# Three chains of A's second output moved between the merges of B's weights

## The chip, the cores and the metric

The kernel runs on one core of one Trainium2 chip. The metric is the device time of one execution in microseconds (us), the median of three runs. Matrix work runs on TensorE (PE in the profile), which writes PSUM banks; ScalarE (ACT) and VectorE (DVE) read these banks and write SBUF; GpSimd (POOL) masks the attention weights in SBUF; SyncE (SP) issues the DMAs.

## The reference

Two independent attention blocks over 2048 tokens of width 640, with 32 heads of width 20; their outputs stand side by side.

```python
def _A_ref(x, wqkv, wo):           # sliding window, W = 256
    q, k, v = split(x @ wqkv)      # (head, token, 20) each
    scores = q @ k.T * 20 ** -0.5
    mask = (i - j >= 0) & (i - j < 256)
    p = softmax(where(mask, scores, -1e9))
    return heads_joined(p @ v) @ wo

def _B_ref(x, wqkv, wo):           # linear attention
    phi = lambda t: where(t > 0, t + 1, exp(t)) + 1e-6
    pq, pk = phi(q), phi(k)
    kv = sum_s(pk[s] outer v[s]);  z = sum_s(pk[s])
    o = (pq @ kv) / (pq @ z + 1e-6)
    return heads_joined(o) @ wo

return concatenate([a, b], axis=-1)
```

## The kernel before, in words

The tokens are cut into four superblocks of 512. Block A's attention is cut into 76 units, numbered 0 to 75 here (units 56 to 75 belong to the last superblock, number 3). A unit is one pass of this loop (L1121): `scores` (L773) multiplies q by k into the four PSUM banks of `S_ps`, ScalarE takes the exponential of all of it into `p`, and GpSimd masks `p`. There is one `S_ps`, so the next unit's scores begin when the exponential has read it. About two units later, for each group of four heads that is complete, `values` (L821) multiplies `p` by v into a bank; VectorE turns that bank (`T`, L847), and a deferred function (`rest`, L856) takes a reciprocal and writes the normalised rows `N` and `Nr`; for the last group of a superblock VectorE turns `Nr` too (L886).

The other matrix work, called the fill, is cut into chains: a chain is the group of matmuls that fills one bank, five for a 512-wide chain (`chain`, L268). Each chain has a due time in `plan`, in units; `fill_of` (L1095) sorts the list by due time and hands the matmuls out in that order. A unit is credited with a fixed number of columns, `rate` (L1119), which is (386520 - 13000 + 32 * 2200) / 76 = 5841; a unit that also does `values` is charged 2200 of them; `take` (L1106) stops at the first matmul at which the credit is used up, and the overdraft goes to the next unit. A chain can so be split by a unit's scores.

All chains, the merges, the denominators and the `values` products use one pool of four banks, named `dense`, taken in rotation: a chain gets the bank that the fourth product before it used, and its first matmul waits until that bank has been read. Who reads it:

- `evac` (L250) copies a bank to SBUF on ScalarE or VectorE. It keeps an account of work for each, `load["A"]` and `load["D"]`, in nominal columns: a copy of n columns adds n + 160, a unit's exponential 1900 to A, a `values` product 1500 to D, a quotient 1400 to D, a denominator 1200 to D, a phi 672 to A and 1700 to D; each unit takes 3000 off both (`pass_tile`, L246). A copy goes to ScalarE if A is less than D + 600, else to VectorE:

```python
to = "A" if load["A"] < load["D"] + AHEAD else "D"
```

- `phi` (L277) takes an exponential on ScalarE at once (L281), and later, when two more banks have begun, two VectorE operations (L285, L288) of which the second reads the bank.
- `b_den` (L709) adds its small constant on VectorE (L727) and then takes a reciprocal.

Each engine works its instructions in the order in which the program gives them out. The pieces that the change touches:

- `b_merge` (L664) multiplies B's summed key-value matrices by B's output weights: ten merges of two matmuls of 320 columns (L673), called merge 0 to merge 9 here, each counted as 640 columns. `b_out` needs them all.
- `a_out(s)` and `b_out(s)` (L892, L760) are the output projections of a superblock: four 512-wide chains, called aout s.0 to s.3 here, and a fifth, s.4, of twenty 128-wide matmuls (`tok_rows`, L472).
- `b_q(s)` (L687) gives five chains of phi(q), here bq s.0 to s.4. Its first call does what is left of the quotients of superblock s - 2 (`quotient(s - 2)`).
- `quotients(s)` (L742) lists four divisions on VectorE (L752), here quot s.0 to s.3. The unit loop takes one from the list in a unit without `values` (L1141), ahead of that unit's fill, and in the others only when the list is long or after unit 68 (L1138). Each is followed by a transposing DMA on SP into `oT_B`.
- `again_x(s)` reloads a superblock of B's x by DMA.

In the last unit, 75, the loop takes 2000 columns of fill, does `values` of group 6, gives out that group's `rest` at once, and then goes on with the fill (L1129 to L1142). After the loop come 5500 columns of fill, `values` of group 7, the PE transposes of `turn_last` (L896), what is left of the fill, and `a_out_last` (L911), the output of A's last superblock.

The due times, sorted, with the times in unit 56 and around it before the change: merges 0 to 9 at 46.34, 47.02 and so on in steps of 0.68 to 52.46; aout 1.0 to 1.4 at 50.66, 51.58, 52.5, 53.42, 54.34; bq 2.0 at 52.5; the denominator of superblock 1 at 53.05; bq 2.1 at 53.5. The work runs behind these due times: merge 5 comes in unit 56.

Of the kernel before, what the change touches and what calls it, by code (L numbers as in the profile page):

```python
# [92 lines left out]
def kernel(  # L93
# [12 lines left out]
    KT = D // P  # L106
# [128 lines left out]
    def settle(all=True):  # L235
        while posts and (all or posts[0][0] <= begun[0]):
            posts.pop(0)[1]()
# [78 lines left out]
    for c in range(KT):  # L316
        m = EXTRA * c
        while m < EXTRA * (c + 1):
            n = min(EXTRA * (c + 1) - m, DH - m % DH)
# [178 lines left out]
    def wo_proj(wt, base, oT, s, col0):  # L498
        osb = op.tile([P, TPS, D], BF16, name="osb")

        def done(tb, ps):
            if tb is None:
                evac(osb[:, :, SB:D], ps)
            else:
                evac(osb[:, tb, 0:SB], ps[:])

        yield from tok_rows(oT, wt, base, done)
        dst = out2[s * SB : (s + 1) * SB, col0 : col0 + D]
        soon(
            lambda: nc.sync.dma_start(out=dst.rearrange("(t p) n -> p t n", p=P), in_=osb[:]), 2  # L510
        )
# [152 lines left out]
    def b_merge():  # L664

        for c in range(KT):
            for lo in (0, D // 2):
                cols = slice(lo, lo + D // 2)
                ps = bank()
                for i in range(2):  # L670

                    at = PAD + (P - GD) * c - i * GD
                    nc.tensor.matmul(  # L673
                        ps[:, 0 : D // 2],
                        lhsT=kv_T[0:GD, c + i, at : at + P],
                        rhs=wo_sb["B"][0 : GH * DH, c + i, cols],
                        start=(i == 0),
                        stop=(i == 1),
                    )
                evac(w_sb["B"][:, c, D + lo : D + lo + D // 2], ps[:, 0 : D // 2], D // 2)  # L680
                yield End(D)
# [210 lines left out]
    def a_out(s):  # L892
        settle()
        yield from wo_proj(wo_sb["A"], 0, oT_A[s], s, 0)
# [137 lines left out]
    plan = []  # L1032

    def at(t0, t1, gen, n):
        for i in range(n):
            plan.append((t0 + (i + 0.5) / n * (t1 - t0), gen, i == n - 1))
# [6 lines left out]
    def parts(t0, t1, n, s):  # L1043
        do(t0, t1, [lambda tb=tb: load_part(n, s, tb) for tb in range(TPS)])
# [30 lines left out]
        at(td, td + 0.1, b_den(s), 1)  # L1075
        do(tx, tx, [lambda s=s: quotients(s)])
    at(46.0, 52.8, b_merge(), 2 * KT)
    for n, s, t0, t1 in (("A", 0, 44.5, 48.5), ("A", 1, 50.2, 54.8), ("B", 0, 54.8, 59.2),
                         ("B", 1, 60.2, 64), ("A", 2, 64.4, 68.2), ("B", 2, 69, 73),
                         ("B", 3, 73, 76)):  # L1080
        at(t0, t1, (a_out if n == "A" else b_out)(s), KT)
    for n, s, t0, t1 in (("B", 1, 5, 9), ("A", 2, 6, 12), ("B", 2, 14, 18), ("B", 3, 19, 25),
                         ("A", 3, 25.5, 33.5)):
        parts(t0, t1, n, s)
# [98 lines left out]
```

## Time and profile before

| | |
|---|---|
| median of three runs | 253.49 us (253.42 to 253.66) |
| profiled execution | 253.07 us |
| its span, first to last instruction | 251.3 us |
| PE busy | 246.6 us, 98% of the span |
| ACT busy | 197.2 us, 78% |
| POOL busy | 186.7 us, 74% |
| DVE busy | 166.9 us, 66% |
| granted TensorE clock | 1.000 |

The span is the time that the timeline's stamps cover; what lies around it in the execution's own time is 1.8 us. A row of a timeline gives the start, the time from the first start to the last end of the merged instructions, the engine, the source line, the operation, output and input, and the count; a number in brackets behind it is the idle time just ahead, with what ended it. A modelled matmul overlaps the next, so the pace of matmuls is read from starts, not from the lengths. Scores stand in the PE timeline under L787, `values` under L834, chains under L271, merges under L673, denominators under L716.

### The profile page before, as it was taken

The numbers are of one execution on the slowest core, as the hardware profiler recorded it, in microseconds if no ns is written. First come the engines' busy times: TensorE is split into PE (matmuls) and PEld (weight loads), VectorE is DVE, ScalarE is ACT, GpSimd is POOL, SyncE is SP. The second block draws the span as 40 slices with busy tenths as digits, with TensorE's granted clock in tenths as the row PEclk, the third lists the DMA queues.
The fourth block names the chain that finished last, engine by engine and source line by source line (L and its number), as shares of the span: only waits on it lengthen the run. The fifth ranks groups of instructions, "written<-read, shape, count | busy, mean of one in ns | idle before, by whom it ended". The sixth has DMA issues, their size and how long they took to land.

```text
span 251.3 us, 8779 instructions
## 1 busy us (share of the span) xinstructions
PE 246.6 (98%) x3730; PEld 141.6 (56%) x3730; DVE 166.9 (66%) x310; ACT 197.2 (78%) x194; POOL 186.7 (74%) x310
## 2 busy tenths in 40 slices
PE   8999999999999999999999999999999999999994
PEld 6644456467755455466545555556555565655573
DVE  1345678767654565686665766666888798859662
ACT  4486789889867788996568877889998998999542
POOL 1227897879877898686878979888887978999800
PEclk9999999999999999999999999999999999999999
DMA  7995597799640342996569394742967398779614
GB/s 219 332 251 156 117 202 135 181 268 140 97 97 3 96 142 37 244 268 163 69 146 154 90 192 78 181 56 46 188 112 159 89 185 173 114 166 143 195 57 154
DMA packets 68412, 37.04 MB, mean 147 GB/s; under 512 B 51605, under 2 KB 67349, under 8 KB 68373
## 3 DMA queue, kind: packets, MB, share of 16 engines
q1 hardware_dynamic: 67685, 35.67, 68.1%
q10 hardware_dynamic: 688, 0.82, 1.0%
q8 instruction: 29, 0.48, 0.8%
q14 instruction: 10, 0.08, 0.1%
HBM read 14.42 MB, written 9.83 MB: 96 GB/s over the span
## 4 chain that ended last, share of the span: by engine, by line
PE 92%; DVE 2%; DMA 2%; ACT 1%; issue 1%; SPq 0%; ACTq 0%
PE dense L271 52%; PE S_ps L787 11%; PE dense L834 9%; PE dense L562 9%; PE dense L406 7%; DMA wA<-in_A_wqkv_dram 2%; PE first L406 1%; PE dense L716 1%; PE dense L673 1%; PE dense L645 1%; DVE phi L288 1%; DVE e L285 0%; ACT e L281 0%; PE dense L901 0%; ACT osb L256 0%
## 5 line engine op out<-in xcount | busy, mean ns | idle before, releaser
L810 POOL TENSOR_SCALAR_AFFINE_SELECT p<-p 128x256 bf16<-128x256 bf16 (+2 forms) x280 | 176.9, 662 | 41.5 <-ACT p L795 40.0
L795 ACT ACTIVATE p<-S_ps 128x2048 bf16<-128x2048 f32 x76 | 142.8, 1879 | 33.8 <-PE S_ps L787 32.0
L271 PE MATMUL dense<-xA,wqk 128*128 128x512 bf16 x200 | 50.9, 380 | 0.0
L787 PEld LDWEIGHTS <-kpad 20*128 20x128 bf16 (+1 forms) x1216 | 21.7, 98 | 29.6 <-issue 26.0
L787 PE MATMUL S_ps<-qpad,kpad 20*65 20x64 bf16 (+3 forms) x1216 | 33.7, 228 | 0.0
L847 DVE STREAM_TRANSPOSE T<-dense 128x512 f32<-128x512 f32 x32 | 22.8, 712 | 15.6 <-PE dense L834 15.4
L285 DVE TENSOR_SCALAR e<-e 128x512 bf16<-128x512 bf16 x40 | 18.6, 465 | 21.4 <-ACT e L281 21.3
L271 PEld LDWEIGHTS <-wqk 128*128 128x128 bf16 x200 | 17.9, 98 | 19.2
L288 DVE SCALAR_TENSOR_TENSOR phi<-dense,e 128x512 bf16<-128x512 f32 x40 | 27.7, 692 | 1.6
L271 PE MATMUL dense<-xB,wB 128*128 128x512 bf16 x100 | 26.3, 380 | 0.0
L834 PE MATMUL dense<-p,vA 128*32 128x64 bf16 (+2 forms) x1216 | 25.9, 231 | 0.0
L271 PE MATMUL dense<-wB,xB 128*128 128x512 bf16 (+1 forms) x160 | 25.9, 300 | 0.0
L562 PE MATMUL dense<-tok,phi 128*128 128x129 bf16 (+1 forms) x160 | 25.5, 300 | 0.0
L271 PE MATMUL dense<-wo,oT 128*128 128x512 bf16 (+4 forms) x165 | 25.1, 296 | 0.0
L281 ACT ACTIVATE e<-dense 128x512 bf16<-128x512 f32 x40 | 23.6, 597 | 1.2 <-PE dense L271 1.0
L271 PE MATMUL dense<-wB,xA 128*128 128x512 bf16 (+1 forms) x160 | 24.3, 299 | 0.0
L406 PE MATMUL dense<-wA,xA 128*128 128x320 bf16 x140 | 23.7, 299 | 0.2 <-DMA wA<-in_A_wqkv_dram 0.2
L834 PEld LDWEIGHTS <-vA 128*32 128x32 bf16 x1216 | 19.4, 97 | 3.8 <-issue 0.8
L256 ACT ACTIVATE osb<-dense 128x512 bf16<-128x512 f32 (+2 forms) x28 | 15.8, 580 | 5.3 <-PE dense L271 5.2
L406 PEld LDWEIGHTS <-xA 128*128 128x128 bf16 x160 | 14.9, 98 | 8.0 <-DVE xA L347 0.4
L864 DVE TENSOR_TENSOR N<-T,recA 128x320 bf16<-128x320 f32 (+1 forms) x28 | 15.5, 553 | 3.3 <-DMA oT<-N 2.3
L752 DVE TENSOR_TENSOR tok<-tok,rden 128x640 bf16<-128x640 bf16 x16 | 17.5, 1093 | 0.2 <-DMA tok<-phi 0.2
(65 smaller groups left out, 195.8 us busy)
## 6 DMA issues: line engine op xcount, KB each, us to landing
out_dram<-osb SPq DMA_DIRECT2D x7, 640.0 KB
x_scr<-xB SPq DMA_DIRECT2D x4, 640.0 KB
tok<-in_B_x_dram SPq DMA_DIRECT2D x4, 640.0 KB
xB<-x_scr SPq DMA_DIRECT2D x4, 640.0 KB
wB<-in_B_wqkv_dram SPq DMA_DIRECT2D x3, 800.0 KB
q_scr<-qpad SPq DMA_DIRECT2D x16, 60.0 KB
k_scr<-kpad SPq DMA_DIRECT2D x16, 60.0 KB
qpad<-q_scr SPq DMA_DIRECT2D x16, 60.0 KB
```

What stands on the lines that cost most here:

```text
L271: nc.tensor.matmul(dst, lhsT=lhs(kt), rhs=rhs(kt), start=(kt == 0), stop=(kt == KT - 1))
L281: nc.scalar.activation(out=view(e), in_=src, func=ACT.Exp)
L285: nc.vector.tensor_scalar(out=e[:], in0=e[:], scalar1=1e-6, scalar2=1.0 + 1e-6, op0=ALU.add, op1=ALU.min)
L288: nc.vector.scalar_tensor_tensor(out=dst, in0=src, scalar=0.0, in1=view(e), op0=ALU.max, op1=ALU.add)
L406: nc.tensor.matmul(ps[:, 0 : hh * DH], lhsT=xt[:, kt, tb * P : (tb + 1) * P], rhs=w_sb["A"][:, kt, i * hh * DH : (i + 1) * hh * DH], start ...
L562: nc.tensor.matmul(out, lhsT=pk[:, tb, c * P : (c + 1) * P], rhs=x[:, tb, lo:hi], start=(i == 0), stop=(i == len(blocks) - 1),)
L752: nc.vector.tensor_tensor(out=vh, in0=vh, in1=rden_of[s][:, tb, :, :].to_broadcast([P, H, DH]), op=ALU.mult)
L787: nc.tensor.matmul(S_ps[0:keys, j, col : col + n], lhsT=k_pad[kb // TPS][rows, g, ko : ko + keys], rhs=q_pad[s][rows, g, q0 : q0 + n], sta ...
L795: nc.scalar.activation(out=p, in_=S_ps[:], func=ACT.Exp, scale=scale)
L810: nc.gpsimd.affine_select(out=dst, in_=v, pattern=[[0, 4], [0, n], [sgn, w]], compare_op=ALU.is_ge, fill=0.0, base=base, channel_multiplie ...
L834: nc.tensor.matmul(O_ps[32 * j : 32 * (j + 1), q0 : q0 + n], lhsT=v_flat[kb // TPS % 3][:, at + j * HV : at + j * HV + 32], rhs=p[:, j, co ...
L847: nc.vector.transpose(out=T.rearrange("p b e -> p (b e)"), in_=O_ps[:])
```

## The change

The due times of A's second output (superblock 1) are no longer spread over 50.2 to 54.8 but written out, 49.6, 50.4, 51.4, 53.4 and 54.3. Nothing else in the kernel's text differs.

```diff
     at(46.0, 52.8, b_merge(), 2 * KT)
-    for n, s, t0, t1 in (("A", 0, 44.5, 48.5), ("A", 1, 50.2, 54.8), ("B", 0, 54.8, 59.2),
+    for n, s, t0, t1 in (("A", 0, 44.5, 48.5), ("B", 0, 54.8, 59.2),
                          ("B", 1, 60.2, 64), ("A", 2, 64.4, 68.2), ("B", 2, 69, 73),
                          ("B", 3, 73, 76)):
         at(t0, t1, (a_out if n == "A" else b_out)(s), KT)
+
+    second = a_out(1)
+    for i, t in enumerate((49.6, 50.4, 51.4, 53.4, 54.3)):
+        plan.append((t, second, i == KT - 1))
```

Sorted by the new times, the stretch of the fill that differs, with the credit's arithmetic giving the units (a chain in parentheses is split, with its matmuls in that unit):

| unit | before | after |
|---|---|---|
| 56 | merge 5, merge 6, aout 1.0, merge 7, aout 1.1 (2 of 5) | aout 1.0, merge 5, aout 1.1 |
| 57 (with `values`) | aout 1.1 (3), merge 8, merge 9, quot 0.3, bq 2.0 (2 of 5) | merge 6, merge 7, aout 1.2 (4 of 5) |
| 58 | bq 2.0 (3), aout 1.2, denominator 1, aout 1.3 (1 of 5) | quot 0.3, aout 1.2 (1), merge 8, merge 9, bq 2.0, denominator 1, aout 1.3 (1 of 5) |

The arithmetic is this. Unit 56 begins with an overdraft of 461, so it may take 5380 columns: before, 640 + 640 + 2560 + 640 + 2 * 512 = 5504 (overdraft 124); after, 2560 + 640 + 2560 = 5760 (overdraft 380). Unit 57 has 5841 - 2200 less the overdraft: before 3517, which takes 3 * 512 + 640 + 640 + 2 * 512 = 3840; after 3261, which takes 640 + 640 + 4 * 512 = 3328 (overdraft 67). Unit 58 ends with the same matmul in both, and the same overdraft of 370; from there on the order of PE's work is the same in both to the end. The reload of x for superblock 3 (`again_x`) stays behind merge 7, so it moves from unit 56 to unit 57; the DMAs keep their order on SP.

## The prediction

> **What bounds the kernel now.** I read the page first, then who waited for whom, then the timelines of PE, DVE and ACT through units 56 to 58 and through the end.
>
> ```profile
> span 251.3 us, 8779 instructions
> PE 246.6 (98%) x3730; PEld 141.6 (56%) x3730; DVE 166.9 (66%) x310; ACT 197.2 (78%) x194; POOL 186.7 (74%) x310
> ...
> L864 DVE TENSOR_TENSOR N<-T,recA 128x320 bf16<-128x320 f32 (+1 forms) x28 | 15.5, 553 | 3.3 <-DMA oT<-N 2.3
> ```
>
> PE is busy 98% of the span (the last row is for the end of the kernel, below). The change adds and removes no matmul, so its worth is only the PE waits that it removes or creates. In the waits of all engines, one row on PE lies in the stretch that is moved:
>
> ```profile
> PE dense L673 <- DVE phi L288: 0.3, 1, 0.3
> ```
>
> The PE timeline of units 56 to 58 shows where:
>
> ```profile
> 177.73 0.43 PE L787 MATMUL S_ps<-qpad,kpad 20*128 20x320 bf16 x12
> 178.09 0.72 PE L673 MATMUL dense<-wo,kv_T 120*128 120x320 bf16 x4
> 178.64 1.24 PE L271 MATMUL dense<-wo,oT 128*128 128x512 bf16 x5
> 180.23 0.43 PE L673 MATMUL dense<-wo,kv_T 120*128 120x320 bf16 x2 [0.34 <-DVE phi L288]
> 180.60 0.59 PE L271 MATMUL dense<-wo,oT 128*128 128x512 bf16 x2
> 181.12 0.46 PE L787 MATMUL S_ps<-qpad,kpad 20*128 20x320 bf16 x20
> ...
> 184.03 0.46 PE L787 MATMUL S_ps<-qpad,kpad 20*128 20x256 bf16 x16
> 184.42 0.82 PE L271 MATMUL dense<-xB,wB 128*128 128x512 bf16 x3
> 185.08 1.24 PE L271 MATMUL dense<-wo,oT 128*128 128x512 bf16 x5
> 186.16 0.65 PE L716 MATMUL dense<-zk,phi 128*128 128x8 bf16 x20
> 186.66 0.38 PE L271 MATMUL dense<-wo,oT 128*128 128x512 bf16 x1
> 186.97 0.43 PE L787 MATMUL S_ps<-qpad,kpad 20*128 20x320 bf16 x12
> ```
>
> Prices on PE, from starts: a 512-wide chain 186.16 - 185.08 = 1.08, so 0.22 a matmul; four merge matmuls 178.64 - 178.09 = 0.55, so 0.27 a merge; a denominator 0.50; the way from a unit's last matmul into the next scores 186.97 - 186.66 - 0.22 = 0.09, say 0.10. At 178.64 a chain of 1.08 should have let merge 7 start at 179.72; it started at 180.23, 0.51 later, and the 0.89 from there to the scores holds 0.27 + 0.43 + 0.10 = 0.80 of work: a stalled start costs about 0.1 more. So the one stall here is worth 0.6 us. Its bank shows the rotation: merge 7 is the fourth product after bq 1.4 (bq 1.4, merge 5, merge 6, aout 1.0, merge 7), and bq 1.4 is read by the phi that ended the wait.
>
> **The change, part by part.** *Unit 56: the wait goes.* After, bq 1.4 is followed by aout 1.0, merge 5, aout 1.1 and the `values` product, which takes its bank well behind 180.23. The unit is 0.36 of scores, 1.08, 0.27, 1.08 and 0.10: unit 57's scores start at 177.73 + 2.89 = 180.62 in place of 181.12.
>
> *Unit 57.* Before it took 184.03 - 181.12 = 2.91; after it does one 512-wide matmul less: 180.62 + 2.91 - 0.22 = 183.31 for unit 58's scores. These need unit 57's exponential:
>
> ```profile
> 180.09 0.79 ACT L256 ACTIVATE wB<-dense 128x320 bf16<-128x320 f32 x2
> 180.72 0.65 ACT L256 ACTIVATE osb<-dense 128x512 bf16<-128x512 f32 x1
> 181.72 1.88 ACT L795 ACTIVATE p<-S_ps 128x2048 bf16<-128x2048 f32 x1 [0.36 <-PE S_ps L787]
> ```
>
> It starts 0.60 behind the scores, 181.22 after, or when ScalarE is done with the copies ahead of it: two of 512 and one of 320 from 180.09, some 1.3 by these rows, 181.4. It ends at 183.3: no stall, or a tenth.
>
> *Unit 58: a new wait.* Products in bank order: aout 1.2, merge 8, merge 9, bq 2.0, denominator 1. The denominator needs aout 1.2's bank. Which engine copies aout 1.2? The accounts stand at A 3452 and D 3040 after unit 57, less 3000 each, plus 1900 for the scores and 1400 for quot 0.3: A 2352, D 1440. 2352 is not under 1440 + 600: VectorE (before: A 3792, D 4532, ScalarE). And VectorE has all this ahead of it, of which the rows of before give the lengths:
>
> ```profile
> 179.49 0.69 DVE L288 SCALAR_TENSOR_TENSOR phi<-dense,e 128x512 bf16<-128x512 f32 x1
> 180.09 0.98 DVE L752 TENSOR_TENSOR tok<-tok,rden 128x640 bf16<-128x640 bf16 x1
> 181.00 0.48 DVE L258 CAST wB<-dense 128x320 bf16<-128x320 f32 x1
> 182.43 0.72 DVE L847 STREAM_TRANSPOSE T<-dense 128x512 f32<-128x512 f32 x1 [0.95 <-PE dense L834]
> 183.16 0.69 DVE L258 CAST osb<-dense 128x512 bf16<-128x512 f32 x1
> 183.76 1.02 DVE L752 TENSOR_TENSOR tok<-tok,rden 128x640 bf16<-128x640 bf16 x1
> 184.71 0.24 DVE L858 RECIPROCAL recA<-T 128x16 f32<-128x16 f32 x1
> 184.99 0.49 DVE L864 TENSOR_TENSOR Nr<-T,recA 128x320 bf16<-128x320 f32 x1
> 185.51 0.71 DVE L886 STREAM_TRANSPOSE oT<-Nr 128x512 bf16<-128x512 bf16 x1
> ```
>
> T starts 182.43 - 181.12 = 1.31 behind the scores: 181.93. Then, start to start: T 0.70, merge 6 and merge 7 (A and D at 3452 and 2080, then 2560: both to VectorE) 0.39 each, being 0.48 less the 0.09 by which 183.16 to 183.76 is shorter than its row, reciprocal 0.28, Nr 0.52, the turn 0.64, quot 0.3, which the loop gives out ahead of aout 1.2's last matmul, 0.95, and aout 1.2 itself 0.69: 4.56, ending at 186.49, and PE starts 0.04 later, as 180.19 to 180.23 did: 186.53. PE is there at 183.31 + 0.39 + 0.22 + 2 * 0.27 + 1.08 = 185.54 or so. Wait: 1.0. From the denominator to the next scores is 186.97 - 186.16 = 0.81, plus 0.1 for the stalled start: 187.4. Against 186.97, with the same matmuls done: **+0.4 us**. The bounds: if ScalarE or VectorE had been free, 186.97 - 0.6 = 186.4, so -0.6; upwards, a slower quotient. All of them:
>
> ```profile
> L752 DVE TENSOR_TENSOR tok<-tok,rden x16: 780/1052/1736, 172.9 to 229.8; 128x640 bf16<-128x640 bf16 x16
> ```
>
> 0.78 to 1.74: the term runs from +0.2 to +1.1. I keep 0.95, near the median, because POOL masks there as it did at 183.76. The Trainium skill, SBUF — State Buffer, section SBUF: two separate sides, has a rule for such spreads: an operation of VectorE with two SBUF inputs and a GpSimd one lock the shared port pair against each other for the whole instruction. By that rule quot 0.3 can be blocked for a whole mask; no row here shows which quotient would be.
>
> *Moved past.* again_x moves one unit; its DMA has until bq 3.0 in unit 64. quot 0.3's DMA into oT_B keeps its place on SP. bq 2.0 ends a unit later or less; its phi finds VectorE idle after. I cost these at nothing; bq 2.0's bank is next used by aout 1.4, over two microseconds after that phi.
>
> *Units 59 to 74.* Aout 1.2 (672) and merges 6 and 9 (480 each) have gone to VectorE and aout 1.1 (672) to ScalarE, so the accounts differ by 960 each, and later copies near the balance flip: aout 1.3, bout 0.3, bout 2.0 and 2.3 to ScalarE, aout 2.4 and bout 2.1 to VectorE. I walked each one's bank; only bout 0.3 bites: 0.48 more on ScalarE ahead of two phi exponentials and of unit 65's, with next to no slack before unit 66's scores and bq 3.3. Bounds 0 and 0.2 (below zero is excluded, since no PE wait stands there to be won): **+0.1 us**.
>
> *The end: the costly flip.* At bout 3.0, the first copy of the last output, A is 2564 and D 1064 + 1500 = 2564 before: ScalarE. After, A is 2948 and D 680 + 1500 = 2180, and 2948 is not under 2780: VectorE. There it stands behind the deferred normalisation, which the last unit gives out first:
>
> ```profile
> 235.58 3.20 PE L271 MATMUL dense<-wB,xA 128*128 128x512 bf16 x14
> ...
> 236.48 0.60 ACT L256 ACTIVATE osb<-dense 128x512 bf16<-128x512 f32 x1 [0.76 <-PE dense L271]
> 236.74 0.70 DVE L864 TENSOR_TENSOR N<-T,recA 128x128 bf16<-128x128 f32 x1
> 237.37 1.25 DVE L864 TENSOR_TENSOR Nr<-T,recA 128x192 bf16<-128x192 f32 x1
> ...
> 238.65 0.69 DVE L258 CAST osb<-dense 128x512 bf16<-128x512 f32 x1
> ...
> 238.70 0.85 PE L834 MATMUL dense<-p,vA 128*32 128x256 bf16 x40
> ```
>
> The ScalarE row at 236.48 is bout 3.0. On VectorE it would take the place at 238.65 and end at 239.34. Bank order: bout 3.0, `values`, bout 3.1, bout 3.2, bout 3.3. The first matmul of bout 3.3, the last of the 14, needs bout 3.0's bank at 238.70 - 0.10 - 0.22 = 238.38 and gets it at 239.38: 1.0, plus 0.1 for the start. The last `values`, the transposes and A's last output all queue behind it on PE: **+1.1 us**, in full. N and Nr take 1.95 here, and 1.1 at the mean of 0.553 in the row above: then it would be 0.25. Below zero is excluded, since no PE wait stands there now.
>
> *Sum.* 0.4 + 0.1 + 1.1 = +1.6 us. The profiled execution took 253.07 (its span 251.3 and 1.8 around it), so 254.7; the median shown is 253.49, 0.4 above it, and so the forecast for it is 255.1.
>
> **The rivals.** *Faster: banks are not bound to the fourth-last product.* Were any freed bank taken, both new waits would find one, and only unit 56's stall would change: -0.6, 252.9. It decides where a bank is free at 185.54 and at 238.38. Against it: merge 7 waited for just the phi of its fourth-last product while PE had nothing else to do.
>
> *The end is hidden.* With N and Nr at their mean, bout 3.0 costs 0.25: +0.75, 254.2; with a somewhat shorter VectorE queue in unit 58 too, no change that can be told. Against it: POOL and the other engines stand to these two operations as before, so their lengths should come again.
>
> *Unit 58 is hidden.* If VectorE's queue is 1.0 shorter there, unit 56's gain stays: -0.5 + 0.1 + 1.1 = +0.7, 254.2.
>
> *A blocked quotient.* With 1.74 for quot 0.3 by the row above, +0.7 on the forecast: 255.8. The median of sixteen is 1.05, so it gets a small chance. The rule of the Trainium skill's SBUF — State Buffer, named above, would make it the ordinary case wherever a long mask has just begun.
>
> **How the numbers follow.** Forecast 0.58, faster 0.08, end hidden 0.12, unit 58 hidden 0.12, blocked quotient 0.10. 0.2% is 0.5 us, about what this measurement can tell from no change: 252.98 to 254.0. Faster by more: 0.08. Within: 0.10, a part of the two hidden cases, which lie 0.2 above that bound. Slower: 0.82. The range drops the faster case and one tenth more: 253.7 (a hidden case, half a microsecond better) to 256.1 (the blocked quotient and the upper end of the rest).
>
> **What would show it.** In the PE timeline after: no bracket at a merge in unit 56; a bracket near 1.0 at the denominator (L716) in unit 58, put down to a VectorE copy; bout 3.3's first matmul, at the end, starting about 1.0 late behind a VectorE copy of osb that follows Nr (L258). It is wrong if PE shows no new idle time, if bout 3.0 is still on ScalarE, or if a wait on a DMA stands among the new ones.

## The result and the profile after

The changed kernel took 254.49 us (median of nine runs, 254.23 to 255.55) beside 253.66 us for the kernel before (nine runs, 253.13 to 255.0): a ratio of 1.0034, 95% interval 1.0017 to 1.005, that is 0.9 us slower (0.4 to 1.3). Forecast were 255.1 us (253.7 to 256.1), +1.6 us, and slower with a chance of 0.82.

The page after; its profiled execution took 255.55 us, the slowest of the nine:

```profile
span 253.8 us, 8780 instructions
PE 246.6 (97%) x3730; PEld 141.7 (56%) x3730; DVE 166.5 (66%) x311; ACT 196.5 (77%) x193; POOL 186.8 (74%) x310
```

PE has the same work, 246.6 us, in a longer span. All of PE's waits after (waited for, total, times, longest):

```profile
PE dense L406 <- DMA wA<-in_A_wqkv_dram: 1.9, 1, 1.9
PE dense L195 <- PEq L1171: 0.8, 1, 0.8
PE dense L716 <- DVE osb L258: 0.8, 1, 0.8
PE dense L834 <- DVE osb L258: 0.5, 1, 0.5
```

The wait of a merge for a phi is gone. In its place stand the denominator (L716) and a `values` product (L834), each waiting for a copy on VectorE. The second row stands in both profiles. The first is another matter: the wait for the first piece of A's v weights, 0.2 us in the profile before. To keep it apart, the spans are cut at the same instructions in both kernels: the scores of units 0, 56, 59 and 75, and the first transpose at the end. The stretches before, then after (stretch, length, PE busy and matmuls, clock, DMA share, GB/s):

```profile
16.65:177.73 161.08, 161.05 (x2519) 1.00 0.68 137
177.73:186.97 9.24, 8.89 (x140) 1.00 0.87 139
186.97:233.25 46.28, 46.28 (x752) 1.00 0.79 149
233.25:239.48 6.23, 6.23 (x129) 1.00 0.52 156
```

```profile
18.25:179.33 161.08, 161.05 (x2518) 1.00 0.68 137
179.33:188.92 9.59, 8.84 (x140) 1.00 0.85 139
188.92:235.17 46.25, 46.25 (x751) 1.00 0.80 149
235.17:241.97 6.80, 6.31 (x130) 1.00 0.45 140
```

Units 0 to 55 took 161.08 us in both. Units 56 to 58 took 9.59 in place of 9.24 (+0.35), units 59 to 74 the same within 0.03, the end from unit 75 to the transposes 6.80 in place of 6.23 (+0.57); what follows took 251.30 - 239.48 = 11.82 and 253.80 - 241.97 = 11.83. The sum is +0.90, the measured +0.9. The opening, ahead of unit 0's scores, took 16.65 us before and 18.25 after. Without it the two profiled executions took 253.07 - 16.65 = 236.42 and 255.55 - 18.25 = 237.30 us, 0.88 apart; if the rest repeats, the medians 253.66 and 254.49 stand for openings of 17.2 us in both (an estimate). So the 1.6 us look like a matter of this one pair of profiles and not of the ratio; the experiments test it.

Units 56 to 58 after, on PE:

```profile
179.33 0.43 PE L787 MATMUL S_ps<-qpad,kpad 20*128 20x320 bf16 x12
...
182.23 0.46 PE L787 MATMUL S_ps<-qpad,kpad 20*128 20x320 bf16 x20
...
184.95 0.46 PE L787 MATMUL S_ps<-qpad,kpad 20*128 20x256 bf16 x16
185.34 0.39 PE L271 MATMUL dense<-wo,oT 128*128 128x512 bf16 x1
185.57 0.71 PE L673 MATMUL dense<-wo,kv_T 120*128 120x320 bf16 x4
186.12 1.24 PE L271 MATMUL dense<-xB,wB 128*128 128x512 bf16 x5
188.11 0.64 PE L716 MATMUL dense<-zk,phi 128*128 128x8 bf16 x20 [0.75 <-DVE osb L258]
188.61 0.38 PE L271 MATMUL dense<-wo,oT 128*128 128x512 bf16 x1
188.92 0.43 PE L787 MATMUL S_ps<-qpad,kpad 20*128 20x320 bf16 x12
```

Unit 56 runs without a stall: 182.23 - 179.33 = 2.90. The chain at 186.12 (bq 2.0) is issued by 187.20, a chain being 1.08; the denominator starts at 188.11, 0.91 later (the bracket's 0.75 counts from the modelled end of the chain). VectorE in that time:

```profile
183.67 0.72 DVE L847 STREAM_TRANSPOSE T<-dense 128x512 f32<-128x512 f32 x1 [0.99 <-PE dense L834]
184.31 0.85 DVE L258 CAST wB<-dense 128x320 bf16<-128x320 f32 x2
185.08 0.23 DVE L858 RECIPROCAL recA<-T 128x16 f32<-128x16 f32 x1
185.35 0.49 DVE L864 TENSOR_TENSOR Nr<-T,recA 128x320 bf16<-128x320 f32 x1
185.87 0.71 DVE L886 STREAM_TRANSPOSE oT<-Nr 128x512 bf16<-128x512 bf16 x1
186.51 0.95 DVE L752 TENSOR_TENSOR tok<-tok,rden 128x640 bf16<-128x640 bf16 x1
187.38 0.68 DVE L258 CAST osb<-dense 128x512 bf16<-128x512 f32 x1
```

It is the queue that the prediction listed, without a gap from 183.67; its last row, aout 1.2, ends at 188.06, and the denominator starts 0.05 later. At the end, on VectorE and PE:

```profile
237.50 3.19 PE L271 MATMUL dense<-wB,xA 128*128 128x512 bf16 x14
...
239.29 1.24 DVE L864 TENSOR_TENSOR Nr<-T,recA 128x192 bf16<-128x192 f32 x1
239.49 0.60 ACT L256 ACTIVATE osb<-dense 128x512 bf16<-128x512 f32 x1 [1.84 <-PE dense L271]
240.46 1.27 DVE L258 CAST osb<-dense 128x512 bf16<-128x512 f32 x2
...
241.19 0.85 PE L834 MATMUL dense<-p,vA 128*32 128x256 bf16 x40 [0.49 <-DVE osb L258]
```

Bout 3.0's copy is the first of the two at 240.46, behind the normalisation. The 14 matmuls, the last of them bout 3.3's first, went through unhindered; it was the `values` product behind them that waited.

### The profile page after: what moved, and what is told of

The parts are those of the page before. It is cut to its first block, busy times and chain, and to the rows that moved or that the text cites. A ratio compares the mean times of both kernels' runs of the same rounds, so it can differ in the third digit from the quotient of the medians.

```text
span 253.8 us, 8780 instructions
## 1 busy us (share of the span) xinstructions
PE 246.6 (97%) x3730; PEld 141.7 (56%) x3730; DVE 166.5 (66%) x311; ACT 196.5 (77%) x193; POOL 186.8 (74%) x310
## 4 chain that ended last, share of the span: by engine, by line
PE 92%; DVE 3%; DMA 2%; issue 0%; SPq 0%; ACT 0%
PE dense L271 52%; PE S_ps L787 11%; PE dense L834 9%; PE dense L562 9%; PE dense L406 8%; DMA wA<-in_A_wqkv_dram 2%; PE first L406 1%; PE dense L716 1%; PE dense L673 1%; DVE Nr L864 1%; PE dense L645 1%; DVE T L847 1%; DVE osb L258 0%; PE dense L901 0%; DVE tok L752 0%
## 5 line engine op out<-in xcount | busy, mean ns | idle before, releaser
L834 PE MATMUL dense<-p,vA 128*32 128x64 bf16 (+2 forms) x1216 | 25.9, 231 | 0.5 <-DVE osb L258 0.5
L834 PEld LDWEIGHTS <-vA 128*32 128x32 bf16 x1216 | 19.6, 97 | 4.2 <-issue 1.3
L256 ACT ACTIVATE osb<-dense 128x512 bf16<-128x512 f32 (+2 forms) x29 | 16.5, 582 | 6.0 <-PE dense L271 5.9
L271 PEld LDWEIGHTS <-oT 128*128 128x128 bf16 x165 | 13.1, 98 | 7.6 <-DVE oT L909 0.2
```

The lines of the kernel that those rows point to most:

```text
L271: nc.tensor.matmul(dst, lhsT=lhs(kt), rhs=rhs(kt), start=(kt == 0), stop=(kt == KT - 1))
L834: nc.tensor.matmul(O_ps[32 * j : 32 * (j + 1), q0 : q0 + n], lhsT=v_flat[kb // TPS % 3][:, at + j * HV : at + j * HV + 32], rhs=p[:, j, co ...
```

## The experiments

Each kernel was timed beside the kernel before. Two theories stood against each other: that the time is two PE waits, for aout 1.2's copy behind quot 0.3 and for bout 3.0's copy behind the normalisation; and that it is lost elsewhere, in the opening or through the order of the merges itself. None of the edits leaves work out. Where an edit moves a copy to another engine, the accounts go on as if it had stayed, so that no later copy flips; in the edits below, `on` is the engine that does it. Added lines shift the line numbers in the rows by a few. In the compiled programs each of these edits moves one VectorE or ScalarE instruction (the combined one two), and all but the last leave every product the bank that it had.

**Bout 3.0 on ScalarE, in the changed kernel.**

```diff
-    def evac(dst, src, n=SB, to=None):
+    def evac(dst, src, n=SB, to=None, on=None):
...
         load[to] += n + COPY
+        to = on or to
...
-                evac(osb[:, tb, 0:SB], ps[:])
+                evac(osb[:, tb, 0:SB], ps[:], on={(D, 3, 0): "A"}.get((col0, s, tb)))
```

> The changed kernel with one copy moved: bout 3.0 is read by ScalarE, the accounts as they were. Theory (two PE waits, unit 58 and the last `values`): only the second goes; the stretch from unit 75's scores to the transposes is 6.23 us again in place of 6.80, and the kernel stands +0.3 us (0.1%) to the kernel before. Rival (the time is lost in the opening, where the profile after has a DMA wait of 1.9 us): the wait at the end goes, the opening stays 1.6 us longer, and the time stays at +0.9 us (0.34%).

Measured: 254.22 us, ratio 1.0027 (0.9998 to 1.0056), or +0.7 us (-0.05 to +1.4); the median of the kernel before was 253.89 here, so the medians differ by 0.3 only. The stretches of units 56 to 58 and of the end:

```profile
179.08:188.63 9.55, 8.78 (x139) 1.00 0.85 140
234.88:241.12 6.24, 6.04 (x128) 1.00 0.50 152
```

The end is back at 6.24, and units 56 to 58 stay long. The time alone can't tell +0.3 from +0.9; the stretch shows that the wait at the end went with this one copy. The opening of this profile was 18.00 us, so that the rival of the opening is still open here.

**Quot 0.3 behind the copies, in the changed kernel.** Unit 58 enters quot 0.3 in the accounts where it stood, but gives it out when bq 2.0 begins, behind the copies of aout 1.2 and merge 9. It is the only instruction that moves, on VectorE alone. `late_quotient` calls what is held back; `False` keeps it from entering the account again.

```diff
     def b_q(s):
+        if s == 2:
+            late_quotient()
         quotient(s - 2)
...
+        elif i == 58:
+            at_s, tb, fn = quotients_due.popleft()
+            assert (at_s, tb) == (0, 3)
+            settle()
+            add_load(d=1400)
+            held_back.append(lambda: fn(tb, False))
```

> The changed kernel with one VectorE instruction moved: quot 0.3 stands behind the copies of aout 1.2 and merge 9, the accounts as they were. Theory: the copy of aout 1.2 ends about 0.9 us earlier, the wait ahead of the denominator goes (0.75 to 0.1 or less), units 56 to 58 take 8.7 us in place of 9.59 (before: 9.24), and the kernel stands +0.0 to +0.1 us to the kernel before, as the wait at the end stays. Rival (the order of the merges, not VectorE's queue, costs the time): units 56 to 58 stay at 9.6.

Measured: 254.04 us, ratio 1.0014 (0.999 to 1.0037): no difference from before that can be told, as expected. Its PE timeline at bq 2.0 and the denominator, and its stretches:

```profile
185.60 1.24 PE L271 MATMUL dense<-xB,wB 128*128 128x512 bf16 x5
186.68 0.65 PE L718 MATMUL dense<-zk,phi 128*128 128x8 bf16 x20
```

```profile
178.81:187.49 8.68, 8.63 (x139) 1.00 0.86 140
233.74:240.53 6.79, 6.10 (x127) 1.00 0.79 203
```

The denominator starts 1.08 behind bq 2.0, with no wait. Units 56 to 58 take 8.68, 0.91 less than in the changed kernel and 0.56 less than before: this is unit 56's stall, won. PE's order is the same as in the changed kernel, so the order on PE is not by itself what cost the time; one VectorE instruction of 0.95 us ahead of the copy was.

**Both edits together.**

> Both edits, bout 3.0 on ScalarE and quot 0.3 behind the copies. Theory: no PE wait is left from unit 56 on, and the kernel is 0.5 to 0.6 us (0.2%) faster than before, what unit 56's wait was worth. Rival (opening): still +0.5 us slower or more. Rival (the waits only move on): a new bracket on PE in units 59 to 75, and no gain.

Measured: 253.32 us, ratio 0.9987 (0.9969 to 1.0004), and once more with its own comparison:

> The kernel with quot 0.3 behind the copies and bout 3.0 on ScalarE once more, for a narrower interval. Theory: units 56 to 58 take 8.7 us, no wait at the end, 0.5 to 0.6 us (0.2%) faster than before. Rival: no difference that can be told.

Measured: 253.52 us, ratio 0.999 (0.9972 to 1.0008). The stretches of the first, then of the second:

```profile
178.66:187.37 8.71, 8.66 (x139) 1.00 0.83 139
233.62:239.85 6.23, 6.03 (x127) 1.00 1.01 239
```

```profile
178.53:187.21 8.68, 8.68 (x142) 1.00 0.86 140
233.45:239.69 6.24, 6.24 (x130) 1.00 0.51 155
```

Both waits are gone and none has come in their place: 0.53 to 0.56 us less than before in the first stretch, nothing lost in the second. Neither interval leaves out "no change", so the times do not show that this kernel beats the one before; the profiles show that it does 0.5 us less waiting. But both intervals, up to 1.0004 and 1.0008, lie below that of the changed kernel, which begins at 1.0017: the times, too, show that the loss goes with the two waits. The rival of the opening asked for +0.5 us or more here, and the intervals end at +0.1 and +0.2. The opening took 17.57 and 17.45 us in these two, 16.65 in the profile before and 18.25 in the one after: it scatters by more than the change is worth.

**Bout 3.0 on VectorE, in the kernel before.** The same edit as the first with "D", in the unchanged order.

> The kernel before with one copy moved: bout 3.0 is read by VectorE, nothing else. Theory (the bank freed first is taken first, so it is the last `values` that waits for this copy): +0.5 to +0.6 us (0.2%), with the wait on the last `values`. Rival (the prediction's, a fixed rotation over four banks): +1.0 to +1.1 us, with the wait on bout 3.3. Rival (the place is hidden): 0.

Measured: 254.42 us, ratio 1.0027 (1.0002 to 1.0052), +0.7 us (0.05 to 1.3). The last `values` and the two stretches:

```profile
240.01 0.85 PE L835 MATMUL dense<-p,vA 128*32 128x256 bf16 x40 [0.49 <-DVE osb L259]
```

```profile
178.49:187.73 9.24, 8.74 (x139) 1.00 0.80 138
234.00:240.79 6.79, 6.10 (x127) 1.00 0.55 167
```

The end takes 6.79, +0.56, with the same bracket as in the changed kernel, and units 56 to 58 are as before. So one copy's engine is the whole of that term, at 0.56 and not at the 1.1 of a fixed rotation. The run shows which product waits, not by which rule the bank was picked.

**Aout 1.2 on ScalarE, in the changed kernel.** The first edit with `(0, 1, 2): "A"`.

> The changed kernel with one copy moved: aout 1.2 is read by ScalarE, the accounts as they were. Theory (what counts is the queue that the copy stands in, not the engine): ScalarE has unit 58's exponential ahead of it, whose row ends 187.43 in the profile after, so the copy would end near 187.9 in place of 188.06: the wait ahead of the denominator shrinks by 0.1 to 0.2 only, units 56 to 58 take 9.4 to 9.5 us, and the kernel stands +0.7 us (0.3%) to the kernel before. Rival (VectorE as such is the cause, as the prediction's lower bound for this term had it: with a free ScalarE the wait goes): units 56 to 58 take 8.7 us.

Measured: 254.68 us, ratio 1.0031 (1.0014 to 1.0048), +0.8 us. The denominator and the stretch; then ScalarE, and VectorE:

```profile
187.31 0.64 PE L717 MATMUL dense<-zk,phi 128*128 128x8 bf16 x20 [0.48 <-DVE wB L259]
```

```profile
178.79:188.12 9.33, 8.85 (x141) 1.00 0.85 140
```

```profile
186.78 0.59 ACT L257 ACTIVATE osb<-dense 128x512 bf16<-128x512 f32 x1
```

```profile
185.90 0.95 DVE L753 TENSOR_TENSOR tok<-tok,rden 128x640 bf16<-128x640 bf16 x1
186.78 0.48 DVE L259 CAST wB<-dense 128x320 bf16<-128x320 f32 x1
```

The wait shrinks by 0.26 us only, and it is not even the wait expected: aout 1.2's copy now ends at 187.37, behind the exponential, and the build gave the denominator the bank of merge 9, whose copy on VectorE, still behind quot 0.3, ends at 187.26. Either bank would have come late: counted from unit 56's scores, aout 1.2's copy ended at 8.58 us on ScalarE and at 8.73 on VectorE, so that one busy queue was hardly better than the other. As the denominator's bank changed with the edit, this is no clean test, and a copy on an idle engine was not tried.

## Why the prediction was right, and where it was not

The direction, the two places and the copies that are waited for were right. Taken by its own steps:

- *Unit 56's wait goes.* Forecast 2.89 us for the unit, measured 2.90.
- *Unit 58's new wait.* Forecast a wait of 1.0 (PE there at 7.81 behind unit 56's scores, released at 8.80), measured 0.91 (7.87 and 8.78). The term of units 56 to 58 was forecast at +0.4 and measured +0.35. The 0.1 for a stalled start did not come: from the denominator to the next scores it is 188.92 - 188.11 = 0.81, as without a stall. Quot 0.3 took the 0.95 that was forecast, but with some luck, as these masks show, which ran beside it from 186.51 to 187.46:

```profile
186.12 0.67 POOL L810 TENSOR_SCALAR_AFFINE_SELECT p<-p 128x512 bf16<-128x512 bf16 x1
186.75 1.67 POOL L810 TENSOR_SCALAR_AFFINE_SELECT p<-p 128x1024 bf16<-128x1024 bf16 x1
```

  Of the 32 quotients in the profiles before and after, the six that began with no mask running took 0.78 us. The others took 0.78 and what was left of the running mask, less about 0.1: quot 0.3 began 0.28 ahead of a mask's end and took 0.95, the two slowest after (1.73) began with 1.05 of a mask left. The mask that followed quot 0.3 took 1.67, against a median of 1.10 for its shape. The Trainium skill's SBUF — State Buffer, section SBUF: two separate sides, says that a VectorE operation with two SBUF inputs and a GpSimd one block each other: whichever starts first holds the shared ports for its whole instruction. The trace agrees, so that the prediction was wrong to say that no row shows which quotient would be blocked: in the profile before, quot 0.3 itself took 1.02 with 0.37 of a mask left. Where in a mask it would fall after was not worked out.
- *Units 59 to 74.* Forecast +0.1 for bout 0.3's flip, measured -0.03. The copy went to ScalarE, but unit 65's exponential began 0.67 us behind its scores in place of 0.60, and ended at 209.01, 0.05 ahead of unit 66's scores: the delay of 0.48 that I took was 0.07.
- *The end.* Forecast +1.1, measured +0.57; this is the term that was mis-sized, and most of the miss of 0.7. The step that failed is "Bank order: bout 3.0, `values`, bout 3.1, bout 3.2, bout 3.3", with the rotation from which it is drawn, which the description of the kernel states too: the pool does not take its banks in rotation. The compiled programs say which bank each product got (both kernels alike but for the numbering; after is shown):

```
bout 3.0  values g6  bout 3.1  bout 3.2  bout 3.3  values g7
    0         1          3         2         1          0
```

  Bout 3.3 took the bank of the `values` product before, which VectorE had read long ago, and the next `values` product took bout 3.0's. PE comes to that product one matmul and one change of operation later, 0.32 us by the terms of the prediction, and bout 3.0's copy began 0.1 earlier than reckoned, at 240.46 or 238.54 on the clock of before; with no price for the start, 1.1 becomes 0.57. In all, 114 of the 217 banks of the kernel before and 121 of those after happen to be those of the fourth-last product. The two that the prediction used in units 56 to 58 are among them: merge 7's before, and the denominator's after. The second was luck: before, the denominator had the bank of the sixth-last product.

  N and Nr came again with 0.70 and 1.24 us, as the prediction argued, and these lengths, too, follow the masks beside them:

```profile
238.56 0.67 POOL L810 TENSOR_SCALAR_AFFINE_SELECT p<-p 128x512 bf16<-128x512 bf16 x1
239.18 1.14 POOL L810 TENSOR_SCALAR_AFFINE_SELECT p<-p 128x1024 bf16<-128x1024 bf16 x1
```

  N began with 0.57 of a mask left, Nr with 1.03. With no mask running N took 0.29 (at 62.86), and Nr would take about 0.3 by the same reckoning, an estimate: without the masks bout 3.0's copy would have come over 1.2 us earlier, and the wait of 0.57 would not have been there. No run moved a mask to test it.

By which rule the build picks a bank stays open. It is not simply the bank that is free first on the chip: in the changed kernel the denominator got aout 1.2's bank, which was read by 188.06, and not merge 8's, which ScalarE had read by 187.75:

```profile
187.32 0.43 ACT L256 ACTIVATE wB<-dense 128x320 bf16<-128x320 f32 x1
```

In the last experiment the denominator got merge 9's bank, two products back, though aout 1.2's copy was given out earlier.

The rivals: the premise of the first, that banks are not bound to the fourth-last product, was right, but not its gain, for the build gave the denominator and the last `values` a bank that was read late. Unit 58 was not hidden, and the end by half, through the bank and not through shorter N and Nr. Quot 0.3 was blocked for 0.17 us only; the slowest one would have cost 1.74 - 0.95 = 0.8, where the prediction has 0.7 (and an upper end of +1.1 for the term, which should be +1.2). The experiments that took one quotient from ahead of a copy, or one copy from behind the normalisation, removed 0.91 and 0.56 us, so that the two waits are shown as causes, each by itself.

## What to carry to other kernels

In this kernel PE was busy 98% of the span; moving chains changed nothing of its work, and the price came from the order in which their banks are read. So list, for each product behind the move, which bank it takes and what stands in front of the copy that frees it. A balance between two engines kept in running accounts carries a small local move far: a difference of 960 nominal columns made in units 56 to 58 came back 17 units later as one copy on the wrong side of a normalisation, and cost 0.57 us, more than the 0.35 of the place that was changed. Read the banks from the compiled program before counting on a rotation, and look in the trace at what the slow operations of that queue stand beside: here their lengths followed the masks on GpSimd.

## What was not expected of the hardware

The opening, before the first scores, took between 16.65 and 18.25 us over eight profiles of kernels that are alike there, with PE's wait for the first v weights going from nothing to 1.9 us. That scatter is larger than every effect in this study, so that the stretches between fixed instructions told the kernels apart where single times could not. The stretches repeat to 0.03 us: units 0 to 55 took 161.08 or 161.09 in all eight. Without its opening the profiled execution of the changed kernel took 0.88 us more than that of the kernel before; with bout 3.0 on ScalarE it was 0.28, with quot 0.3 moved -0.01, and with both -0.55 and -0.60.
